# The first load of wq as 16 whole rows, the other 112 rows by columns

## The chip, the cores and the metric

The kernel runs on one core of a Trainium2 chip. Time is device microseconds (us) of that core, from the program's start to its end; the figure for a kernel is the median of several runs. Beside it stands a profile, one execution recorded by the hardware profiler, whose span runs from the first instruction to the last.

## The reference

One decoding step of an attention block and a small MLP in parallel, on one token x of 512 numbers, all in float32:

```
xn = layernorm(x)
q  = xn @ wq                                  # 512 x 4096, 32 heads of 128
scores = q . k_cache * 128 ** -0.5            # 8 kv heads, 65536 positions, 4 q heads share a kv head
o  = softmax(scores) . v_cache
y  = x + o @ wo + relu(xn @ w1) @ w2          # wo 4096 x 512, w1 512 x 1792, w2 1792 x 512
```

k_cache and v_cache hold 268 MB each; wq and wo hold 8.4 MB each, w1 and w2 3.7 MB each. Nearly all of the work is to bring them into the core once.

## The kernel before

The caches are cut into 32 chunks of 16384 positions, four to a kv head. A chunk of k is a tile `kt` of 128 partitions with rows of 64 KB, a chunk of v the like tile `vt`. TensorE multiplies a chunk of k by the four q heads (L313), VectorE transposes the scores out of the accumulator (L366) and finds their maximum, ScalarE takes exponentials (L256), and TensorE multiplies by v (L292). There is one `kt` and one `vt`, so that k comes in while v is used and the other way round.

All large loads are issued by SyncE in one order, written out by hand: wq, w1, the first k, then v and k in turn, then wo, w2 and the store. Before each k and v SyncE takes a count from a semaphore (`kfree`, `vfree`) that says that the tile is free. The rows of a load are shared out over 16 DMA engines, and each engine takes what is queued for it in order.

The projection q = xn @ wq uses the path of the scores: wq is laid out as a tile of 128 partitions with rows of 16384 numbers (64 KB) and is loaded into `kt`; the normalized x, laid out over 128 partitions, stands in `qpad` as the weights. wq comes in three loads by columns, of 4096, 4096 and 8192 columns (`WQ_CUTS`), each over all 128 partitions. Each adds 16 to a semaphore of its own when all of it has landed (`WQ_SEMS`):

- the first adds to `ends`. GpSimd computes the end of the layernorm (L208 to L212), takes 16 from `ends` (L213), then copies xn to `qpad` and releases TensorE through `q` (L214);
- the second adds to `k`, for which TensorE waits (L308) before the eight rounds of matmuls of the loop at L309. A round is 2048 columns, so rounds 0 and 1 use the first load, 2 and 3 the second, 4 to 7 the third;
- the third adds to `wq2`. VectorE waits for it after its first transpose (L367 to L368) and only then lets TensorE go on to rounds 4 to 7. With the last transposes it also adds to `kfree` (L365), so that SyncE can issue the first k into the same tile (L161, L162).

The first load (L151) is issued ahead of the section in which the engines run by their own semaphores; the others (L157 to L159) follow inside it, after a meeting of the engines. w1 (L160) stands behind them; GpSimd multiplies and adds it up (L217 to L224), for TensorE's sums at L281. The vector x itself comes in by ScalarE's own queue (L234, L235), in 128 rows of 16 bytes and one row of 2 KB, through the same DMA engines.

Of the kernel before, what the change touches and what calls it, by code (L numbers as in the profile page):

```python
# [40 lines left out]
WQ_CUTS = [4096, 4096, 8192]  # L41
WQ_SEMS = ["ends", "k", "wq2"]
# [2 lines left out]
W2_SUM = 12  # L45
W2_ROWS = 10
PASSES = 3


def take(e, sem, n=1):  # L50

    return e.sem_inc(sem, -n).wait_op(sem, n, "sem-ge")  # L52
# [7 lines left out]
def attention_and_mlp_kernel(  # L60
# [12 lines left out]
    sp, pe, dve, act, pool = nc.sync, nc.tensor, nc.vector, nc.scalar, nc.gpsimd  # L73
    scale = float(DH) ** -0.5

    def sbuf(name, *shape):
        return nc.alloc_sbuf_tensor(name, list(shape), F32).ap()
# [3 lines left out]
    def sem(name):  # L81
        if name not in sems:
            sems[name] = nc.alloc_semaphore(name)
        return sems[name]

    def after(ins, name, n=1):

        return ins.wait_op(sem(name), n, "sem-ge")

    kt = sbuf("kt", P, CHUNK)  # L90
# [47 lines left out]
    wq_row = wq[0].rearrange("p a n -> p (a n)")  # L138
# [9 lines left out]

    load = sp.dma_start(kt[:, : WQ_CUTS[0]], wq_row[:, : WQ_CUTS[0]]).then_inc(sem(WQ_SEMS[0]), 16)  # L151
    tc.no_tile_sem_insts.add(load.ins.name)
    tc.add_to_no_dep_group("first", load.ins)
    tc.declare_fence(pool.nop().ins, group="first")
    section = ctx.enter_context(ExitStack())
    inside = section.enter_context(tc.tile_critical(sync_engine=mybir.EngineType.Pool, no_gpsimd_drain=True))  # L156
    for i in range(1, len(WQ_CUTS)):  # L157
        cut = slice(wq_at[i], wq_at[i + 1])
        sp.dma_start(kt[:, cut], wq_row[:, cut]).then_inc(sem(WQ_SEMS[i]), 16)  # L159
    sp.dma_start(wt, w1_row).then_inc(sem("w1"), 16)  # L160
    take(sp, sem("kfree"))  # L161
    sp.dma_start(kt, k[0, 0]).then_inc(sem("k"), 16)  # L162
# [8 lines left out]
    for i in range(len(WO_CUTS)):  # L171
        cut = slice(wo_at[i] * D, wo_at[i + 1] * D)
        sp.dma_start(kt[:, cut], wo_row[:, cut]).then_inc(sem(f"wo{i}" if i else "k"), 16)
    sp.wait_ge(sem("hT"), 1)
    for i in range(len(W2_CUTS)):
        cut = slice(w2_at[i] * D, w2_at[i + 1] * D)
# [7 lines left out]
    def link(ins):  # L184

        if chain[0]:
            after(ins, "pool", chain[0])
        chain[0] += 1
        return ins.then_inc(sem("pool"), 1)
# [20 lines left out]
    link(pool.tensor_scalar(st[:, 6:7], st[:, 6:7], -0.5, 1.5, op0=ALU.mult, op1=ALU.add))  # L210
    link(pool.tensor_mul(st[:, 7:8], st[:, 5:6], st[:, 6:7]))
    link(pool.tensor_scalar_mul(xn, xc, st[:, 7:8]))  # L212
    take(pool, sem("ends"), 16)  # L213
    after(pool.tensor_copy(qpad[:, :XA], xn), "pool", chain[0]).then_inc(sem("q"), 1)  # L214
    f = DFF_ALL
    w1_of = [wt[:, a * f : (a + 1) * f] for a in range(XA)]
# [54 lines left out]
    with nc.body("turns", valid_engines=[pe.engine]):  # L271
# [3 lines left out]
        with pe.If(t > 1):  # L275
            after(pe.transpose(pma[:GROUP, :P], m, ident), "d2p").then_inc(sem("p2d"), 1)  # L276
            after(pe.matmul(pmb[:, :GROUP], ones[:GROUP, :], dg, start=True, stop=True), "d2p", 2).then_inc(sem("p2d"), 1)  # L277

            with pe.Fori(0, PASSES):
                for c in range(CT):  # L280
# [175 lines left out]
```

## Time and profile before

| | |
|---|---|
| median of 3 runs | 1303.14 us (1303.03 to 1303.14) |
| span of the profiled execution | 1301.3 us, 1.8 below the median; the profile gives no other time of this execution |
| moved by DMA | 561.02 MB, mean 431 GB/s |
| DMA engines' share of the span | 99.7% |
| PE, PEld, DVE, ACT, POOL busy | 60%, 18%, 21%, 6%, 3% of the span |
| first, second and third load of wq, issued to landed | 7.2, 11.5 and 20.8 us |
| w1, issued to landed | 28.9 us |
| k and v chunks, issued to landed (median) | 24.1 and 29.3 us |

PE is TensorE's matmuls, PEld its weight loads, DVE VectorE, ACT ScalarE, POOL GpSimd, SP SyncE; SPq and ACTq are the instructions by which SyncE and ScalarE issue DMAs. A line such as `L313 PE MATMUL banks<-kt,qpad ... x32 [3.03 <-PEq L52]` gives the line of the kernel, the engine, the operation, output and inputs, how many are merged, and in brackets how long the engine had been idle and what ended that. The DMA share and the GB/s of a window count a row by the time at which it starts.

### The profile page before, as it was taken

The numbers are of one execution on the slowest core, as the hardware profiler recorded it, in microseconds if no ns is written. First come the engines' busy times: TensorE is split into PE (matmuls) and PEld (weight loads), VectorE is DVE, ScalarE is ACT, GpSimd is POOL, SyncE is SP. The second block draws the span as 40 slices with busy tenths as digits, with TensorE's granted clock in tenths as the row PEclk, the third lists the DMA queues.
The fourth block names the chain that finished last, engine by engine and source line by source line (L and its number), as shares of the span: only waits on it lengthen the run. The fifth ranks groups of instructions, "written<-read, shape, count | busy, mean of one in ns | idle before, by whom it ended". The sixth has DMA issues, their size and how long they took to land.

```text
span 1301.3 us, 13055 instructions
## 1 busy us (share of the span) xinstructions
PE 774.9 (60%) x5474; PEld 231.1 (18%) x5474; DVE 274.8 (21%) x466; ACT 76.2 (6%) x299; POOL 34.8 (3%) x30
## 2 busy tenths in 40 slices
PE   3365674665576456566555566666567466557557
PEld 1111121111121111121111121111112111112112
DVE  2211222211222220222220122221122221122222
ACT  1000000000000000000000000000000000000000
POOL 1900000000000000000000000000000000000000
PEclk9677877776887777786776777677777777777779
DMA  9999999999999999999999999999999999999998
GB/s 403 451 419 451 419 451 419 435 435 419 451 419 451 419 451 419 449 421 423 447 419 451 419 451 419 451 419 435 435 419 451 419 451 419 451 419 443 427 420 370
DMA packets 11236, 561.02 MB, mean 431 GB/s; under 512 B 1505, under 2 KB 1505, under 8 KB 1890
## 3 DMA queue, kind: packets, MB, share of 16 engines
q1 hardware_dynamic: 11088, 561.00, 99.7%
q10 hardware_dynamic: 146, 0.00, 0.0%
q8 instruction: 1, 0.02, 0.0%
q14 instruction: 1, 0.01, 0.0%
HBM read 560.99 MB, written 0.00 MB: 431 GB/s over the span
## 4 chain that ended last, share of the span: by engine, by line
issue 94%; DMA 3%; POOL 2%; SPq 0%; PE 0%; DVE 0%; POOLq 0%
DMA wt<-w 3%; POOL wt L219 1%; POOL wt L224 0%; POOL wt L222 0%; POOL wt L223 0%; SPq L177 0%; SPq L159 0%; PE banks L339 0%; DVE ysb L417 0%; SPq L151 0%; POOL hT L226 0%; SPq L452 0%; POOLq L156 0%
## 5 line engine op out<-in xcount | busy, mean ns | idle before, releaser
L313 PE MATMUL banks<-kt,qpad 128*32 128x512 f32 x2176 | 310.0, 733 | 311.1 <-PEq L52 308.7
L292 PE MATMUL banks<-vt,probs 128*16 128x512 f32 x2048 | 271.3, 690 | 82.1 <-PEq L52 82.1
L366 DVE STREAM_TRANSPOSE tr<-banks 128x1024 f32<-128x1024 f32 x136 | 170.0, 1250 | 471.4 <-PE banks L313 466.8
L313 PEld LDWEIGHTS banks<-kt,qpad 128*32 128x32 f32 x2176 | 84.5, 131 | 509.6 <-issue 496.3
L281 PE MATMUL banks<-wt,ones 128*1 128x448 f32 x768 | 121.3, 786 | 0.0
L292 PEld LDWEIGHTS banks<-vt,probs 128*16 128x16 f32 x2048 | 68.4, 108 | 298.4 <-issue 298.4
L392 DVE COPY o_sb<-banks 128x512 f32<-128x512 f32 x32 | 22.1, 692 | 455.3 <-PE banks L292 455.3
L254 ACT ACTIVATE corr<-diff 128x8 f32<-128x8 f32 x32 | 6.7, 208 | 1179.8 <-ACTq L52 1179.8
L256 ACT ACTIVATE probs<-tr,nb_new 128x128 f32<-128x128 f32 x128 | 65.3, 521 | 0.0
L276 PE MATMUL banks<-ident,m 128*4 128x128 f32 x32 | 9.7, 303 | 78.9 <-DVE m L384 78.9
L302 PE MATMUL banks<-sel,o_sb 128*128 128x4 f32 x256 | 32.8, 252 | 18.7 <-PEq L52 18.7
L302 PEld LDWEIGHTS banks<-sel,o_sb 128*128 128x128 f32 x256 | 31.0, 191 | 20.6 <-issue 20.6
L226 POOL TENSOR_SCALAR hT<-ysum 128x14 f32<-128x14 f32 x1 | 0.3, 257 | 1220.7 <-DVE ysum L404 1220.7
L384 DVE TENSOR_REDUCE m<-tr 128x4 f32<-128x512 f32 x32 | 32.2, 1006 | 2.9
L281 PEld LDWEIGHTS banks<-wt,ones 128*1 128x1 f32 x768 | 20.2, 100 | 58.9 <-issue 58.4
L277 PE MATMUL banks<-dg,ones 4*128 4x4 f32 x64 | 15.4, 309 | 20.0 <-DVE dg L387 20.0
L256 ACT ACTIVATION_READ_ACCUMULATOR probs<-tr,nb_new 128x1 f32 x128 | 24.0, 187 | 0.0
L276 PEld LDWEIGHTS banks<-ident,m 128*4 128x4 f32 x32 | 2.6, 81 | 108.0 <-DVE m L384 108.0
L219 POOL TENSOR_SCALAR wt<-wt,xn 128x1792 f32<-128x1792 f32 x4 | 19.1, 4797 | 16.5 <-DMA wt<-w 16.5
L277 PEld LDWEIGHTS banks<-dg,ones 4*128 4x128 f32 x64 | 12.6, 245 | 27.1 <-DVE dg L387 27.1
L299 PEld LDWEIGHTS banks<-part_sum,ones 128*128 128x128 f32 x64 | 9.5, 188 | 27.2 <-issue 27.2
L395 DVE TENSOR_TENSOR lo_run<-lo_run,banks 128x8 f32<-128x8 f32 x32 | 5.2, 163 | 40.0 <-DVEq L52 40.0
(69 smaller groups left out, 91.1 us busy)
## 6 DMA issues: line engine op xcount, KB each, us to landing
kt<-wq SPq DMA_DIRECT2D x2, 2048.0 KB, 9.3
kt<-wq SPq DMA_DIRECT2D x1, 4096.0 KB, 20.8
kt<-wo SPq DMA_DIRECT2D x1, 4096.0 KB, 15.5
kt<-wo SPq DMA_DIRECT2D x2, 2048.0 KB, 22.2
wt<-w SPq DMA_DIRECT2D x1, 3584.0 KB, 28.9
wt<-w SPq DMA_DIRECT2D x1, 1536.0 KB, 9.5
wt<-w SPq DMA_DIRECT2D x1, 1024.0 KB, 11.7
kt<-k SPq DMA_DIRECT2D x32, 24.1
```

What stands on the lines that cost most here:

```text
L219: last = pool.tensor_scalar_mul(w1_of[a], w1_of[a], xn[:, a : a + 1])
L256: last = act.activation(probs[:, :, g], tr[:, :, g], AF.Exp, bias=nb_new[:, g : g + 1], scale=scale, accum_out=part_sum[:, g : g + 1],)
L276: after(pe.transpose(pma[:GROUP, :P], m, ident), "d2p").then_inc(sem("p2d"), 1)
L277: after(pe.matmul(pmb[:, :GROUP], ones[:GROUP, :], dg, start=True, stop=True), "d2p", 2).then_inc(sem("p2d"), 1)
L281: ins = pe.matmul(hrow[32 * c : 32 * c + 1, :], ones[:, :1], hb[:, :, 32 * c : 32 * c + 32], start=True, stop=True,)
L292: last = pe.matmul(acc[c : c + WIDE * GROUP, :], probs[:, b : b + WIDE, :].rearrange("p b g -> p (b g)"), vt[:, b * DH : (b + WIDE) * DH], ...
L299: pe.matmul(lo_new[:, 0, :], ones, part_sum, start=True, stop=True).then_inc(sem("vfree"), 1)
L302: last = pe.matmul(lo_new[:, 1, :], o_sb[:, b, :], sel[:, b, :], start=(b == 0), stop=(b == WIDE - 1),)
L313: last = pe.matmul(pair[s // 2 % 2][32 * c : 32 * c + 32, s % 2 * 512 : s % 2 * 512 + 512], qpad, kb[:, s * 16 : s * 16 + 16, c, :], start ...
L366: ins = after(dve.transpose(tr2[:, s * 1024 : (s + 1) * 1024], pair[s % 2]), "p2d", s + 1)
L384: dve.reduce_max(m, tr.rearrange("p b i -> p i b")[:, :GROUP, :], axis=AX.X).then_inc(sem("d2p"), 1)
L392: after(dve.tensor_copy(o_sb.rearrange("p b d -> p (b d)"), acc), "p2d", 7).then_inc(sem("d2p"), 1)
```

## The change

The first load takes 16 whole rows: partitions 0 to 15 of `kt` with all 16384 columns, 64 KB each, 1 MB in all. The three loads by columns remain, with the same cuts, but bring only partitions 16 to 127. The first of them is issued inside the section, in front of the two others, and adds to `ends` as well, from which GpSimd now takes 32. All of wq still comes in once, into the same places.

```diff
+FIRST = 16
...
-    load = sp.dma_start(kt[:, : WQ_CUTS[0]], wq_row[:, : WQ_CUTS[0]]).then_inc(sem(WQ_SEMS[0]), 16)
+    load = sp.dma_start(kt[:FIRST, :], wq_row[:FIRST, :]).then_inc(sem(WQ_SEMS[0]), 16)
     tc.no_tile_sem_insts.add(load.ins.name)
...
+    sp.dma_start(kt[FIRST:, : WQ_CUTS[0]], wq_row[FIRST:, : WQ_CUTS[0]]).then_inc(sem(WQ_SEMS[0]), 16)
     for i in range(1, len(WQ_CUTS)):
         cut = slice(wq_at[i], wq_at[i + 1])
-        sp.dma_start(kt[:, cut], wq_row[:, cut]).then_inc(sem(WQ_SEMS[i]), 16)
+        sp.dma_start(kt[FIRST:, cut], wq_row[FIRST:, cut]).then_inc(sem(WQ_SEMS[i]), 16)
...
-    take(pool, sem("ends"), 16)
+    take(pool, sem("ends"), 32)
```

On SyncE, at the start of the program, these are the loads before, with the partitions and columns of each and the semaphore that it waits for:

```order
L151 DMA kt<-wq 128x4096
L452 UNCONDITIONAL_BRANCH [waits Pool_sequencer_49]
L159 DMA kt<-wq 128x4096
L159 DMA kt<-wq 128x8192
L160 DMA wt<-w 128x7168
L162 DMA kt<-k 128x16384 [waits kfree]
```

And these are the loads after (the lines of the changed kernel, one or two further down):

```order
L152 DMA kt<-wq 16x16384
L454 UNCONDITIONAL_BRANCH [waits Pool_sequencer_49]
L158 DMA kt<-wq 112x4096
L161 DMA kt<-wq 112x4096
L161 DMA kt<-wq 112x8192
L162 DMA wt<-w 128x7168
L164 DMA kt<-k 128x16384 [waits kfree]
```

One load stands more between the meeting and w1, and four loads of wq are ahead of w1 in place of three. No other engine has an instruction more, fewer or elsewhere.

## The prediction

> **What bounds the kernel now.** I read the page's DMA part first, then the stream between the first and the last chunk, then the first 60 us by engine queue. The second column of the queue line is MB moved, the third the share of the time of sixteen DMA engines:
>
> ```profile
> DMA packets 11236, 561.02 MB, mean 431 GB/s; under 512 B 1505, under 2 KB 1505, under 8 KB 1890
> q1 hardware_dynamic: 11088, 561.00, 99.7%
> ```
>
> SyncE's queue q1 moves all of the 561 MB and keeps the sixteen engines busy for 99.7% of the span. The same view for the stretch from 60 to 1260 us, where only k and v move, has one rate from slice to slice:
>
> ```profile
> GB/s 419 443 430 419 454 419 446 428 419 454 419 450 424 419 454 419 450 424 419 454 419 452 422 419 454 419 452 422 419 454 419 452 422 419 454 419 452 422 419 454
> DMA packets 8928, 520.10 MB, mean 433 GB/s; under 512 B 992, under 2 KB 992, under 8 KB 992
> q1 hardware_dynamic: 8928, 520.10, 100.1%
> ```
>
> There is no idle time in the middle that could absorb a delay from the start. What the stream loses in its first microseconds arrives at the end whole; what it wins there as well. So the question is how long the first 12 MB (wq, then w1) take. The timeline of SyncE's queue (start, duration, instruction) and the wait chain's w1 piece (start, duration):
>
> ```profile
> 0.73 0.39 SPq L151 DMA_DIRECT2D kt<-wq  x1
> 1.34 0.83 SPq L159 DMA_DIRECT2D kt<-wq  x2
> 2.22 0.69 SPq L160 DMA_DIRECT2D wt<-w  x1
> 26.46 0.33 SPq L162 DMA_DIRECT2D kt<-k  x1
> 27.18 0.34 SPq L165 DMA_DIRECT2D vt<-v  x1
> 2.22 28.86 DMA wt<-w
> ```
>
> w1 lands at 2.22 + 28.86 = 31.08 us. The first k chunk is issued at 26.46, 4.6 us before that, so the stream does not stop between them. The first line below is the landing time of that k issue (last three figures), the second TensorE's first weight load on it:
>
> ```profile
> DMA to landing us min/median/max: 24.0/24.0/24.0
> 50.53 0.44 PEld L313 LDWEIGHTS banks<-kt,qpad 128*32 128x32 f32 x8 [25.17 <-issue]
> ```
>
> k lands at 50.46, 19.4 us after w1. A chunk is 128 rows of 64 KB, eight to an engine, so **one engine takes 19.4 / 8 = 2.42 us for a row of 64 KB** and 0.61 for one of 16 KB. The stream's start, in windows (length, then the busy times of PE, PEld, DVE, ACT and POOL, clock, DMA share, GB/s):
>
> ```profile
> 0.00:1.70 1.70, 0.00 (x0) 0.00 (x0) 0.17 (x1) 0.00 (x0) 0.76 (x9) 1.00 0.00 0
> 1.70:6.70 5.00, 0.00 (x0) 0.00 (x0) 3.47 (x1) 1.28 (x1) 1.50 (x8) 1.00 0.98 370
> ```
>
> No data row starts before 1.70 us, 1.0 after the first issue; the next 5 us run at 370 GB/s, 5 x (1 - 370/433) = 0.7 us behind the later pace. These 1.7 us are all that a better start could win.
>
> **The change part by part.** *The first load* was 128 rows of 16 KB (2 MB) and becomes 16 rows of 64 KB (1 MB), partitions 0 to 15 of `kt`, one per engine. Floor: each engine writes its row at its own pace, 2.42 us, and nothing is lost. But no row of this trace shows a large load to fewer than 128 partitions. The even rate of about 433 GB/s, whatever is loaded, says that something fixed and evenly divided holds the stream, and the receiving side may be that as well as the engines: sixteen paths into the memory with eight partitions each fit the rows just as well. Then sixteen neighbours lie on fewer paths than sixteen engines. Ceiling: eight neighbours to a path, two paths, 8 x 2.42 = 19.4 us, the time of a whole chunk. The steps between are two to a path (4.8 us) and four (9.7 us). The trace cannot choose. I take four: it is one step from the ceiling, whose row is the only one here in which 64 KB rows fill a set of partitions, and two from the floor, for which there is only the rate of an engine that has a path to itself. Cost 9.7 - 2.42 = **7.3 us**; ends 0 and 17.0. If four rows share a path evenly, all sixteen engines are held, and nothing behind them on the queue starts earlier, since an engine takes its rows in order.
>
> The Trainium skill, SBUF — State Buffer, section on the DMA port swizzle, says that 16 ports receive DMA writes, that partitions 0 to 15 reach 4 of them, and gives 104 GB/s measured for 1 MiB to these partitions. By it the 1 MiB would take 10.1 us, and the term be 7.7 us. No row of before shows such a load.
>
> *The other 112 rows* come in three loads by columns: 7 rows to each engine instead of 8, 7 x 2.42 = 16.9 us at full pace. Floor: 16.9, so that the whole of wq takes 2.42 + 16.9 = 19.4 as before. With paths, a share of seven consecutive rows no longer coincides with one path: shares start at 16, 23, 30 and so on, straddle two sets of four or more, and at any moment some engines meet on a path and others have one alone. A row met by one other engine takes twice as long. Ceiling: the slowest engine meets another on all seven rows, +16.9; floor 0. A middle can be counted: the partitions 16, 23, 30, ... 121 that sixteen engines write first fall into sets of four that are mostly different, yet those engines that meet stay together for some rows, since both move on by one partition at a time, and an engine that falls behind then meets the w1 rows of those ahead. The load counts only when its slowest engine is done. I take half of the slowest engine's rows as met: 16.9 x 1.5 - 16.9 = **8.5 us**, nearest to neither end.
>
> *The queue.* One issue more on SyncE, 0.33 to 0.44 us by the rows of L159 to L162; w1 is then issued at about 2.6. That is covered: the 16-row load, from 1.7 us on, keeps each engine busy until 4.1 at the earliest, and the 112-row load is issued at 1.34 as L159 was, so its rows are there at 2.4. If the cover were gone, 0.4 us. The next issue, k at 26.46, waits for `kfree` in any case. GpSimd's wait for the first load now wants 32 in place of 16, no instruction more; behind it stand its copy of xn to `qpad` and TensorE's first matmuls, so their cover is to be looked at. First the load of x among the DMA issues (KB, us to landing), then the timeline:
>
> ```profile
> xT<-x ACTq DMA_DIRECT2D x1, 2.0 KB, 8.2
> ```
>
> ```profile
> 9.27 0.21 ACT L240 ACTIVATE xc<-xT 128x4 f32<-128x4 f32 x1 [6.03 <-DMA xT<-x]
> 14.52 0.19 POOL L214 COPY qpad<-xn 128x4 f32<-128x4 f32 x1
> 15.00 5.17 PE L313 MATMUL banks<-kt,qpad 128*32 128x512 f32 x32 [3.03 <-PEq L52]
> 22.66 1.25 DVE L366 STREAM_TRANSPOSE tr<-banks 128x1024 f32<-128x1024 f32 x1 [2.90 <-DMA kt<-wq]
> 26.45 1.25 DVE L366 STREAM_TRANSPOSE tr<-banks 128x1024 f32<-128x1024 f32 x1 [0.58 <-PE banks L313]
> ```
>
> x lands at 9.2 us, and TensorE has the first half of wq done at 20.2; then VectorE waits for the third load, until 22.66, and 3.8 us later SyncE issues k. Its 2 KB take 8.2 us, so I take it that its eight short rows per engine take turns with wq's rows. With a 64 KB row of 9.7 us ahead they begin at 1.7 + 9.7 = 11.4 and need eight turns of 0.61 to 1.22 us: x lands at 16.3 to 21.2, TensorE is done 20.2 - 9.2 = 11.0 later, at 27.3 to 32.2. The third load lands at 11.4 + 16.9 = 28.3 with no meetings and 36.8 with my half. So x's chain stays hidden behind the third load, by a microsecond or more. k follows 3.8 us after that load, and w1 still streams for 31.08 - 22.6 = 8.5 us behind it: the slowest engine does not run dry (8.5 against 3.8 + 1.0), and engines ahead of it only idle.
>
> *Sum*: 7.3 + 8.5 = 15.8 us. The profiled span of 1301.3 becomes 1317.1; the median of the runs, 1303.14, lies 1.8 above the span and becomes **1318.9**. The likeliest case's own range follows from the second term's ends: 1303.1 + 7.3 = 1310.4 to 1303.1 + 7.3 + 16.9 = 1327.3.
>
> **The rivals.** *No sharing (not slower).* The engines are the bound, and each writes its row at 2.42 us wherever it goes. For it: 433 GB/s is equally well sixteen engines at 27 GB/s. Against it: nothing in the trace, only that it needs the receiving side to have room to spare. It decides from the point where the 16-row load's last row ends by 4.2 us. Time: 1303.1, or down to 1301.4 if all 1.7 us of the start were won; that is 0.13%, below the 0.2% (2.6 us) that a measurement of this kernel can tell from no change. So faster is nearly excluded.
>
> *Eight rows to an engine.* 112 = 14 x 8: if the loads keep eight rows to an engine, two engines idle and fourteen have nine rows of 64 KB: +2.42 us, 1305.6. For it: eight is what every load has now. The Trainium skill, DMA: Bandwidth & Descriptors, section on why a DMA increments its semaphore by 16, says that the largest count up to 16 that divides the rows is used, which gives 16 engines with seven rows; no row of before shows it.
>
> *Rows dealt one by one.* If row i goes to engine i mod 16, all engines write to sixteen neighbours at each moment, and all of wq comes at the pace of four paths: 4 x 19.4 = 77.6, +58.2, 1361.3. The trace gives no partition of a single row, so nothing speaks for it or against it but that contiguous shares are simpler.
>
> *Two to a path.* The first load takes 4.8 (+2.4), the meetings a quarter of the rows (+4.2): 1309.7.
>
> **How the numbers follow.** Sharing by four with contiguous shares 0.73, two to a path 0.07, one by one 0.07, no sharing 0.10, eight to an engine 0.03. The last two count as within 0.2%, but for 0.01 of a won start and a tail of the 1305.6 above the bound: slower 0.87, same 0.12, faster 0.01. The range 1306 to 1328 holds the first two cases and leaves out no sharing, eight to an engine and one by one, 0.2 in all.
>
> **What would show it.** The window of the first 10 us: about 110 GB/s after 1.7 us if four share, still about 370 if none do. The landing of the first load: 9.7 us or more after its first row, against 2.4. x's landing near 16 to 21 us instead of 9.2. The third load's landing, VectorE's wait for it and the issue of k all later by the same 14 to 16 us, and w1's landing near 47; from there on every row as before, only shifted, with the stream at 433 GB/s. If x's chain and not the third load ends VectorE's wait, my cover was wrong; if w1's and k's landings are more than 20 us apart, the slowest engine ran dry. The prediction is wrong if partitions 0 to 15 take rows as fast as any, or if seven-row shares never meet, or meet nearly always.

## The result and the profile after

The changed kernel takes 1323.06 us, median of 5 runs (1322.65 to 1325.13), against 1303.14 (1303.03 to 1303.83) before: 1.0153 times as long, 95% interval 1.0141 to 1.0166, or 19.9 us more. The profiled execution's span went from 1301.3 to 1320.9 us, 19.6 more.

The page of the changed kernel, its DMA part:

```profile
DMA packets 11220, 561.02 MB, mean 425 GB/s; under 512 B 1521, under 2 KB 1521, under 8 KB 1906
q1 hardware_dynamic: 11072, 561.00, 99.6%
```

The bytes are the same and the engines are still reckoned busy for 99.6% of the span, but at 425 GB/s. An engine that is held up on the way into the memory counts as busy: over the first ten microseconds of data below, from 1.7 to 11.7 us, the share comes to 1.08 (the mean of 1.72 and 0.45) and the rate to 131 GB/s. The stretch from 80 to 1280 us shows where the loss is not:

```profile
GB/s 448 424 424 448 424 441 433 424 443 426 441 433 428 439 426 439 435 424 443 426 439 435 424 443 426 439 435 426 441 426 439 435 424 443 426 439 435 424 446 424
DMA packets 8928, 520.10 MB, mean 433 GB/s; under 512 B 992, under 2 KB 992, under 8 KB 992
```

433 GB/s, as before. So all of it is in the start, which the windows show (the last figure is GB/s by the rows that start in a window):

```profile
1.70:6.70 5.00, 0.00 (x0) 0.00 (x0) 3.47 (x1) 1.28 (x1) 1.51 (x8) 1.00 1.72 210
6.70:11.70 5.00, 0.00 (x0) 0.00 (x0) 0.00 (x0) 0.00 (x0) 0.00 (x0) 1.00 0.45 53
11.70:16.70 5.00, 1.17 (x4) 1.00 (x4) 0.00 (x0) 1.44 (x9) 0.00 (x0) 1.00 0.88 246
16.70:21.70 5.00, 0.00 (x0) 0.00 (x0) 0.16 (x1) 1.89 (x3) 1.26 (x6) 1.00 1.02 282
21.70:26.70 5.00, 0.11 (x4) 0.14 (x8) 0.00 (x0) 0.00 (x0) 0.00 (x0) 1.00 1.08 279
26.70:31.70 5.00, 4.80 (x32) 1.14 (x31) 1.25 (x1) 0.00 (x0) 0.00 (x0) 1.00 1.04 295
31.70:36.70 5.00, 0.00 (x0) 0.00 (x0) 0.00 (x0) 0.00 (x0) 0.00 (x0) 0.93 1.00 256
```

The sixteen rows of the first load all start in the first window (210 GB/s over 5 us is 1.05 MB) and then nothing starts until 9.8 us. In the trace's records of single rows these sixteen took 8.0 to 9.3 us each, and the last ended 9.6 us after the first had begun; an engine with a free way takes 2.42. Then come 25 us of the 112-row loads at 246 to 295 GB/s in place of 433. None of their rows runs at full pace: those of 16 KB take 0.75 to 2.50 us, half of them over 0.95, in place of 0.61, and those of 32 KB take 2.0 us in the median, in place of 1.21. The timeline, with the answers to the rows quoted of before:

```profile
0.73 0.40 SPq L152 DMA_DIRECT2D kt<-wq  x1
1.35 0.32 SPq L158 DMA_DIRECT2D kt<-wq  x1
1.73 1.11 SPq L161 DMA_DIRECT2D kt<-wq  x2
2.88 0.44 SPq L162 DMA_DIRECT2D wt<-w  x1
13.38 0.20 ACT L242 ACTIVATE xc<-xT 128x4 f32<-128x4 f32 x1 [10.14 <-DMA xT<-x]
19.82 0.19 POOL L216 COPY qpad<-xn 128x4 f32<-128x4 f32 x1 [1.26 <-POOLq L53]
26.59 4.91 PE L315 MATMUL banks<-kt,qpad 128*32 128x512 f32 x32 [10.51 <-PEq L53]
40.97 6.25 PE L315 MATMUL banks<-kt,qpad 128*32 128x512 f32 x32 [9.46 <-DVEq L370]
41.01 1.25 DVE L368 STREAM_TRANSPOSE tr<-banks 128x1024 f32<-128x1024 f32 x1 [9.90 <-DMA kt<-wq]
47.42 0.35 SPq L164 DMA_DIRECT2D kt<-k  x1
49.35 19.12 POOL L221 TENSOR_SCALAR wt<-wt,xn 128x1792 f32<-128x1792 f32 x4 [29.34 <-DMA wt<-w]
70.13 0.46 PEld L315 LDWEIGHTS banks<-kt,qpad 128*32 128x32 f32 x8 [23.84 <-issue]
```

VectorE's wait for the third load ends at 41.0 in place of 22.7 (+18.3). w1 has landed at 49.3 (2.88 and 46.4 to landing) in place of 31.1 (+18.2). The first k is there at 70.0 in place of 50.5 (+19.5), and from there nothing is lost or won to the end. So the 19.6 us divide into 7.1 for the first load (9.56 - 2.42), about 11.1 for the 112-row loads (18.2 - 7.1), and a third part of 1.3 that opens between w1 and k: they land 20.7 us apart, where 19.4 is the time of a chunk.

### The profile page after: what moved, and what is told of

The parts are those of the page before. It is cut to its first block, busy times and chain, and to the rows that moved or that the text cites. A ratio compares the mean times of both kernels' runs of the same rounds, so it can differ in the third digit from the quotient of the medians.

```text
span 1320.9 us, 13056 instructions
## 1 busy us (share of the span) xinstructions
PE 772.9 (59%) x5474; PEld 231.0 (17%) x5474; DVE 279.1 (21%) x466; ACT 76.1 (6%) x299; POOL 34.9 (3%) x30
## 3 DMA queue, kind: packets, MB, share of 16 engines
q1 hardware_dynamic: 11072, 561.00, 99.6%
## 4 chain that ended last, share of the span: by engine, by line
issue 92%; DMA 5%; POOL 2%; SPq 0%; PE 0%; DVE 0%; POOLq 0%
DMA wt<-w 5%; POOL wt L221 1%; POOL wt L226 0%; POOL wt L225 0%; POOL wt L224 0%; PE banks L341 0%; SPq L161 0%; SPq L179 0%; DVE ysb L419 0%; SPq L152 0%; PE banks L354 0%; SPq L158 0%; POOL hT L228 0%; SPq L454 0%; POOLq L157 0%
## 5 line engine op out<-in xcount | busy, mean ns | idle before, releaser
L283 PE MATMUL banks<-wt,ones 128*1 128x448 f32 x768 | 116.5, 759 | 0.0
L304 PE MATMUL banks<-sel,o_sb 128*128 128x4 f32 x256 | 32.8, 251 | 18.7 <-PEq L53 18.7
L304 PEld LDWEIGHTS banks<-sel,o_sb 128*128 128x128 f32 x256 | 31.0, 191 | 20.5 <-issue 20.5
L386 DVE TENSOR_REDUCE m<-tr 128x4 f32<-128x512 f32 x32 | 32.2, 1005 | 2.9
L283 PEld LDWEIGHTS banks<-wt,ones 128*1 128x1 f32 x768 | 20.0, 98 | 54.3 <-issue 53.7
L279 PE MATMUL banks<-dg,ones 4*128 4x4 f32 x64 | 14.4, 293 | 19.9 <-DVE dg L389 19.9
## 6 DMA issues: line engine op xcount, KB each, us to landing
wt<-w SPq DMA_DIRECT2D x1, 3584.0 KB, 46.4
wt<-w SPq DMA_DIRECT2D x1, 1536.0 KB, 11.7
```

Of the source, the lines that this page charges most:

```text
L283: ins = pe.matmul(hrow[32 * c : 32 * c + 1, :], ones[:, :1], hb[:, :, 32 * c : 32 * c + 32], start=True, stop=True,)
L304: last = pe.matmul(lo_new[:, 1, :], o_sb[:, b, :], sel[:, b, :], start=(b == 0), stop=(b == WIDE - 1),)
L386: dve.reduce_max(m, tr.rearrange("p b i -> p i b")[:, :GROUP, :], axis=AX.X).then_inc(sem("d2p"), 1)
```

## The experiments

### Is it the partitions that make the 16-row load slow?

Each of these kernels is the one before with one load more (one of the three lines marked c16, s4 and s8), behind w1, into the idle tile `vt`, where it is never used; SyncE waits for it ahead of the first v. Source and size of the three are the same, and only the sixteen partitions written differ. This kernel and the others with a load added to the kernel before were executed once each; the kernel before, executed beside them, took 1302.9 to 1303.8 us, so that differences of several microseconds are clear.

```diff
     sp.dma_start(wt, w1_row).then_inc(sem("w1"), 16)
+    sp.dma_start(vt[0:16, :], wq_row[0:16, :]).then_inc(sem("extra"), 16)       # c16
+    sp.dma_start(vt[0:64:4, :], wq_row[0:16, :]).then_inc(sem("extra"), 16)     # s4
+    sp.dma_start(vt[0:128:8, :], wq_row[0:16, :]).then_inc(sem("extra"), 16)    # s8
     take(sp, sem("kfree"))
     sp.dma_start(kt, k[0, 0]).then_inc(sem("k"), 16)
+    sp.wait_ge(sem("extra"), 16)
```

> The kernel before with one load more, issued behind w1 and ahead of the first k: 16 rows of 64 KB of wq into partitions 0 to 15 of vt, whose content is never used. By the sharing theory (four neighbouring partitions to one receiving path) the load takes 4 x 2.42 = 9.7 us of the stream: it lands 9.7 us after w1, k 29 us after w1 in place of 19.4, and the span is 1301.3 + 9.7 = 1311.0. By the rival that the slow first load was an effect of the program's start, and not of the partitions, it takes 2.4 us and the span is 1303.7.

> As c16, the same 16 rows of wq, but into partitions 0, 4, 8 ... 60. If sets of four neighbours have a path each and no two sets share one, every row has a path to itself: 2.4 us, span 1303.7. If a partition and the one 32 further on share a path, two rows meet: 4.8 us, 1306.1. If eight neighbours share a path, two rows meet as well: 4.8 us. If the source, one block of 1 MB in memory, was what was slow, it takes 9.7 us as c16, 1311.0.

> As c16, the same 16 rows of wq, but into partitions 0, 8, 16 ... 120. If eight neighbours share a path, or four do and no two sets share, each row has a path to itself: 2.4 us, span 1303.7. If sets of four 32 apart share a path (but not those 64 apart), two rows meet: 4.8 us, 1306.1. If all sets 32, 64 and 96 apart share one, four rows meet: 9.7 us. If the source was what was slow, 9.7 us, 1311.0.

The landing of the added load after its issue at 2.9 us, in c16, s4 and s8:

```profile
DMA to landing us min/median/max: 38.0/38.0/38.0
```

```profile
DMA to landing us min/median/max: 33.5/33.5/33.5
```

```profile
DMA to landing us min/median/max: 33.8/33.8/33.8
```

w1 landed at 31.1 us before, so the added load took 9.8 us in c16 (2.9 + 38.0 - 31.1), 5.3 in s4 and 5.6 in s8. The records of the sixteen rows, from the first start to the last end, give 9.5, 5.3 and 5.6. The spans are 1311.3, 1307.1 and 1306.9 us, 10.0, 5.8 and 5.6 more than before. The start of the program has no part in it, since this load comes 30 us into the run; nor has the source, which is the same. What counts is where the rows go: neighbours in sets of four share a path, and sixteen rows spread over the partitions still meet in pairs. In s4 no two rows are in one set of four, so either eight neighbours share a path or sets do. s8 excludes eight neighbours, which would have taken 2.4 us; it allows pairs of sets 32 apart, but not all sets 32, 64 and 96 apart.

### Which sets share a path

The same added load with 64 rows, four to an engine, at three starts:

```diff
+    sp.dma_start(vt[0:64, :], wq_row[0:64, :]).then_inc(sem("extra"), 16)       # r64_0
+    sp.dma_start(vt[32:96, :], wq_row[0:64, :]).then_inc(sem("extra"), 16)      # r64_32
+    sp.dma_start(vt[36:100, :], wq_row[0:64, :]).then_inc(sem("extra"), 16)     # r64_36
```

> As r112, but 64 rows into partitions 0 to 63, four whole rows to an engine, so that each engine's share is one set of four neighbours. Without sharing, or if no two sets share a path: 4 x 2.42 = 9.7 us. If a set and the one 32 further on share a path, two engines meet on each path all the time: 19.4 us, lands 19.4 after w1, span 1320.7. If rows were dealt one by one: 38.7 or more.

> As r64_0, the same 64 rows of wq, but into partitions 32 to 95. If a set of four shares a path with the set 32 further on (0 to 31 with 32 to 63, 64 to 95 with 96 to 127), these sixteen sets have sixteen paths: 9.7 us, lands 9.7 after w1, span 1311.0, half of r64_0. If it's sets 64 apart that share, this one and r64_0 both take 9.7; if a load of 64 rows is slow for its count of rows, both take 19.4.

> As r64_32, the same 64 rows of wq, four to an engine, but one set of four further on, into partitions 36 to 99. If all that counts is that two rows in flight are on one path, fourteen engines write at 2.42 us a row, and only the two whose sets are 64 to 67 and 96 to 99 meet, at 4.8 to 5.1: the stream runs near 400 GB/s for the first 9.7 us of the load, and the slowest engine ends 19.4 to 20.5 us after w1, span about 1321.5. If each engine has a path of its own, and every row to another path than the engine's own is slow, all engines are slow, and the stream runs at 210 to 230 GB/s for all of the load, about 20 us, span about 1322 as well: the rate in the windows tells them apart.

Windows of r64_0, then r64_32, then r64_36:

```profile
35.00:40.00 5.00, 0.00 (x0) 0.00 (x0) 0.00 (x0) 0.00 (x0) 5.00 (x2) 0.50 1.02 210
40.00:45.00 5.00, 0.00 (x0) 0.00 (x0) 0.00 (x0) 0.00 (x0) 5.00 (x2) 0.50 1.02 210
```

```profile
35.00:40.00 5.00, 0.00 (x0) 0.00 (x0) 0.00 (x0) 0.00 (x0) 5.00 (x2) 0.50 1.12 485
40.00:45.00 5.00, 0.00 (x0) 0.00 (x0) 0.00 (x0) 0.00 (x0) 5.00 (x2) 0.50 1.15 498
```

```profile
35.00:40.00 5.00, 0.00 (x0) 0.00 (x0) 0.00 (x0) 0.00 (x0) 5.00 (x2) 0.50 1.01 393
40.00:45.00 5.00, 0.00 (x0) 0.00 (x0) 0.00 (x0) 0.00 (x0) 5.00 (x2) 0.50 1.20 367
45.00:50.00 5.00, 0.00 (x0) 0.00 (x0) 0.00 (x0) 0.00 (x0) 5.00 (x2) 0.50 1.24 367
50.00:55.00 5.00, 0.00 (x0) 0.00 (x0) 0.00 (x0) 0.00 (x0) 4.92 (x3) 0.50 0.53 184
```

The same 4 MB run at half the pace into partitions 0 to 63 and at full pace into 32 to 95 (a window counts whole rows at their start, hence figures above 433). The landings, 48.8 and 38.0 us after the issue at 2.9, are 20.6 and 9.8 us behind w1's 31.1; spans 1322.2 and 1311.5. So a set of four shares its path with the set 32 further on, and 32 to 95 is a stretch in which no two do: sixteen paths in all, eight partitions to each. The Trainium skill, SBUF — State Buffer, section on the DMA port swizzle, has this map, with 0 to 63 on eight ports. It agrees with these six runs, r64_36 included; for its 196 GB/s, measured with 1 MiB into 64 partitions, 204 stand here (4.19 MB in 20.6 us).

r64_36 was to tell whether a path belongs to an engine, and it does not. The trace names no engine for a row; I follow an engine from the end of one row to the start of the next. Fourteen of the engines write their rows at 2.4 to 2.8 us, though with four rows to each in order none of them is on the set that it had in r64_32. Only two engines, by the map those with sets 64 to 67 and 96 to 99, take 4.5 to 5.1. That part came as expected, with 393 GB/s in the first full window. The end did not: the load lands 26.0 us behind w1 (2.9 + 54.2 - 31.1), not 19.4 to 20.5, and the span is 1328.5. In the records of rows the two late engines go on into a time in which others already load k, a third engine comes onto their path, and three rows at once take 7.1 to 8.1 us each. So the two that were late were made later by one that was ahead.

### Why the 112-row loads are slow

```diff
+    sp.dma_start(vt[16:128, :], wq_row[0:112, :]).then_inc(sem("extra"), 16)    # r112
+    sp.dma_start(vt[0:112, :], wq_row[0:112, :]).then_inc(sem("extra"), 16)     # r112_0
+    sp.dma_start(vt[32:128, :], wq_row[0:96, :]).then_inc(sem("extra"), 16)     # r96_32
```

> The kernel before with one load more behind w1: 112 rows of 64 KB of wq into partitions 16 to 127 of vt, whose content is never used. At full pace it takes 7 x 2.42 = 16.9 us and lands 16.9 us after w1. By the theory that shares of seven rows meet on the paths, whatever was ahead of them, it lands 25 to 29 us after w1 (the changed kernel took 28.5), and the span is 1301.3 + 25 to 29. By the rival that the meetings in the changed kernel came from the engines being staggered by its first load, it lands 17 to 20 us after w1, span 1318 to 1321. Rows dealt one by one would take 68 us.

> As r112, the same 112 rows of wq, but into partitions 0 to 111. If it is the start at 16 that makes all shares meet, this takes less than r112's 34.8 us; if a share of seven rows is what does it, since it fits no set of four wherever it starts, it takes 30 to 36 us again, span 1331 to 1337. Full pace would be 16.9 us, 1318.2.

> As r112 and r64_32, but 96 rows into partitions 32 to 127, six to an engine. Full pace is 6 x 2.42 = 14.5 us behind w1, span 1315.8. If any share that is not one whole set of four is slow as the shares of seven were (34.8 us, 2.06 times full pace), it takes 25 to 30 us, span 1326 to 1331. If only an odd share is slow, it takes 14.5 to 17 us.

The windows of r112, and then the landing in r96_32:

```profile
35.00:40.00 5.00, 0.00 (x0) 0.00 (x0) 0.00 (x0) 0.00 (x0) 5.00 (x2) 0.50 1.05 288
40.00:45.00 5.00, 0.00 (x0) 0.00 (x0) 0.00 (x0) 0.00 (x0) 5.00 (x2) 0.50 0.79 236
45.00:50.00 5.00, 0.00 (x0) 0.00 (x0) 0.00 (x0) 0.00 (x0) 5.00 (x2) 0.50 0.93 223
50.00:55.00 5.00, 0.00 (x0) 0.00 (x0) 0.00 (x0) 0.00 (x0) 4.92 (x2) 0.50 1.12 249
```

```profile
DMA to landing us min/median/max: 58.6/58.6/58.6
```

r112's load lands 32.8 us behind w1's 31.1 (2.9 + 61.0 - 31.1), r112_0's 32.2 (3.0 + 60.3), r96_32's 30.4 (2.9 + 58.6), against 16.9, 16.9 and 14.5 at the full pace of the engines. The spans are 1335.6, 1334.5 and 1332.3. The rival falls: without any late load ahead, with all engines in step, 112 rows run at half that pace, and worse than in the changed kernel. Neither the start at 16 nor the odd share matters, since six rows to an engine from partition 32 are as slow. r112 comes out above what was expected, r112_0 within it and r96_32 a little above. (The 34.8 us that the last two expectations give for r112 is not its landing, which is 32.8.)

Part of this follows from the map. The sixteen partitions left out in r112 or r112_0 lie on four paths and halve those; the other twelve paths still get eight rows each. In r96_32 eight paths still get eight. At 2.42 us a row, none of the three loads can take less than 8 x 2.42 = 19.4 us, the time of a whole chunk, however its rows are dealt. That is an estimate from the map, and 11 to 13 us of the three times stay above it.

What was not expected is how even it is. In r96_32 every row of every engine takes 4.3 to 5.1 us, from the first to the last; in r112 all sixteen first rows take 4.3 to 4.8. If engine e had rows 6e to 6e + 5 or 7e to 7e + 6 of the load, as in the forecast, only two pairs in each would have met at the start by the map that the loads of 64 rows show, and the others would have had 2.42. So either the rows of these loads are not dealt in such consecutive shares, or something slows them that the map does not have; the place of the rows in the source, for one, was not varied here. Dealing one by one, with four rows to a path, is excluded by its 9.7 us a row. If two engines took neighbouring rows side by side, every row would meet one other: 6 x 4.84 = 29.0 us for r96_32, which fits its rows, and 7 x 4.84 = 33.9 for r112, which fits in total, but not its third and fourth rows, 2.7 to 3.5 us on fourteen of the engines. The trace does not give a row's partition, and no run tells how they are dealt. It stays open.

### The first load alone

```diff
-    load = sp.dma_start(kt[:, : WQ_CUTS[0]], wq_row[:, : WQ_CUTS[0]]).then_inc(sem(WQ_SEMS[0]), 16)
+    load = sp.dma_start(vt[:16, :], wq_row[:16, :]).then_inc(sem(WQ_SEMS[0]), 16)
...
+    sp.dma_start(kt[:, : WQ_CUTS[0]], wq_row[:, : WQ_CUTS[0]]).then_inc(sem(WQ_SEMS[0]), 16)
     for i in range(1, len(WQ_CUTS)):
...
-    take(pool, sem("ends"), 16)
+    take(pool, sem("ends"), 32)
```

> The changed kernel's first part alone: the first load is 16 rows of 64 KB of wq into partitions 0 to 15 (of vt, where they are not used), and behind it wq comes in by three loads over all 128 partitions as before, so that 1 MB is loaded twice. By the theory that the change's cost is 7.1 us of sharing in the first load and some 11 us of the 112-row loads, this one costs the first load alone, 9.6 us: w1 lands at 40.7 in place of 31.1, the span is 1310.9, the time 1312.7, and 1.3 us more if k comes late behind w1 as in the changed kernel. By the rival that the late first load unsettles the engines, whatever follows it, so that the loads behind it slow down as they did in the changed kernel, w1 lands near 50 and the time is near 1322.

1313.16 us (1312.60 to 1314.17), 1.0076 times before (1.0059 to 1.0093); span 1312.4. w1 lands at 40.8 (issued at 3.0, 37.8 to landing), k 20.7 us later, at 61.5. The rival falls: behind the slow first load, loads of 128 rows run as they always did. Of the 11.1 us in the span, 9.7 are there when w1 lands, and 1.3 come up between w1 and k, as in the changed kernel. The profiled execution is the longest of the four; two others have spans of 1310.8 and 1310.9 us, what the first load costs alone. They have no trace, so whether k was on time in them is not known.

### The late k

In the changed kernel SyncE issues k 6.4 us after the third load's wait ends (47.42 against 41.01), before 3.8 (26.46 against 22.66). In between are TensorE's rounds 4 to 7, which take 6.25 us in place of 3.64, and TensorE's granted clock is the reason that the windows offer (changed kernel; the clock is the third figure from the end):

```profile
31.00:36.00 5.00, 0.50 (x8) 0.00 (x0) 0.10 (x1) 0.00 (x0) 0.00 (x0) 1.00 1.03 269
36.00:41.00 5.00, 0.03 (x4) 0.03 (x5) 0.00 (x0) 0.00 (x0) 0.00 (x0) 0.50 0.91 275
41.00:46.00 5.00, 5.00 (x24) 1.15 (x28) 2.50 (x2) 0.00 (x0) 0.00 (x0) 0.50 1.01 436
46.00:48.00 2.00, 1.22 (x12) 0.20 (x4) 0.59 (x1) 0.00 (x0) 0.00 (x0) 0.93 0.67 287
```

TensorE ends the first half at 31.5, and from 36 on the clock is 0.50, while it waits; the second half begins at that clock. Before, the wait was from 20.2 to 22.6, and the clock stayed at 1.00:

```profile
19.00:22.00 3.00, 1.17 (x12) 0.14 (x4) 0.76 (x1) 0.00 (x0) 0.00 (x0) 1.00 1.01 436
22.00:27.00 5.00, 3.64 (x32) 0.96 (x32) 3.05 (x3) 0.00 (x0) 0.00 (x0) 1.00 0.95 407
```

The Trainium skill, TensorE: Matmul & The Clock Gate, section on the HAM clock gate, says that half the clock is the state after an idle window of about 3.4 us, and full clock comes after a busy one. The 4.5 us until the fall agree with that, but the fall does not always take 3.4 us of idling: in the kernel before, TensorE ends its second half at 26.3, and the clock falls at 28.4.

That the late issue costs time shows in the records of rows. w1's last rows end on the sixteen engines between 47.4 and 48.7 us; k's first rows start only at 48.4 to 49.7, so most engines stood idle, and these rows then took 2.9 to 3.5 us in place of 2.42. In first16 k was late in the same way: issued 6.5 us after the third load's wait ended (38.97 against 32.43), with the clock at 0.61 in the window from 30 to 35 us. Two runs bear on it:

```diff
+    sp.dma_start(vt[:, :4096], wq_row[:, :4096]).then_inc(sem("extra"), 16)     # cover, behind w1
...
+            if s == ROUNDS // 2:                                                # busy, TensorE's loop of rounds
+                with pe.If(t < 1):
+                    for _ in range(36):
+                        pe.matmul(acc[:16, :P], ident[:, :16], ident, start=True, stop=True)
```

In cover SyncE also waits for the added load ahead of the first v, as in the runs above.

> The changed kernel with a load of 128 rows of 16 KB (2 MB, 4.84 us of the stream) into vt more, behind w1 and ahead of the first k, never used. If k came late in the changed kernel, since TensorE's half clock put off its issue until w1's cover was used up, the longer cover takes that back: k lands 19.4 us after the added load, which lands 4.8 after w1, so the span is 1320.9 + 4.8 - 1.3 = 1324.4. If k was not late but slow for another reason (its first rows took 2.9 to 3.5 us in place of 2.42), it is late again: k lands 20.7 us after the added load, and the span is 1325.7.

> The changed kernel, with 36 matmuls of 128 columns more on TensorE (into rows of acc that the next chunk writes anew) in the first turn, between rounds 3 and 4, while it waits for the third load of wq. If TensorE's half clock is why SyncE issued k 6.4 us after that load had landed, in place of 3.8, then a busy TensorE keeps the clock at 1.00, k is issued 3.8 to 4.2 us after the landing, lands 19.4 us after w1 in place of 20.7, and the time falls by about 1.3 us from the changed kernel's 1323.1. If the late k has another cause, it lands 20.7 us after w1 as before and the time stays.

In busy the same windows read as the first fence shows, and the timeline around the issue of k as the second:

```profile
31.00:36.00 5.00, 5.00 (x52) 3.65 (x43) 0.86 (x1) 0.00 (x0) 0.00 (x0) 1.00 0.99 252
36.00:41.00 5.00, 4.18 (x39) 3.47 (x36) 0.00 (x0) 0.00 (x0) 0.00 (x0) 1.00 0.90 227
41.00:46.00 5.00, 3.50 (x32) 0.96 (x32) 2.50 (x2) 0.00 (x0) 0.00 (x0) 1.00 1.00 424
```

```profile
42.54 1.25 DVE L372 STREAM_TRANSPOSE tr<-banks 128x1024 f32<-128x1024 f32 x1 [10.68 <-DMA kt<-wq]
46.34 0.35 SPq L164 DMA_DIRECT2D kt<-k  x1
```

The clock stays at 1.00, k is issued 3.8 us after the wait's end, and lands 19.4 us after w1 (46.34 + 23.7 = 70.0 against 3.0 + 47.6 = 50.6); its first rows take 2.42 us. So it was the clock that made k late in the profiled execution. The median, 1321.18 us, is 1.9 below the changed kernel's 1323.06, but the ratios to before, 1.0136 (1.0119 to 1.0153) and 1.0153 (1.0141 to 1.0166), overlap: the time alone would not show it. Busy's profiled execution is the longest of its four (span 1323.7, the others 1319.1 to 1319.4); its third load landed 1.5 us later than the changed kernel's, so the 112-row loads do not take the same time in every execution.

In cover k lands at 73.1 us, 19.4 after the added load's 53.7 (3.4 + 50.3), so with a longer cover the late issue costs nothing there either. But the span is 1326.0, not 1324.4: from k's landing to the end it takes 2.0 us longer than the changed kernel, 1.2 of them for the final store, which took 2.6 us to land in place of 1.4; the rest is not accounted for. The time, 1327.71 us (1326.87 to 1333.06), tells nothing apart.

## Why the prediction was right

Slower was forecast, at 1318.9 us in a range of 1306 to 1328, and 1323.06 was measured. Its steps:

- *The first load, +7.3 us by four rows to a path*: right. It measured 7.1, and c16, s4 and s8 show that it is the set of four partitions that does it. The choice of four among one, two, four and eight was not backed by a row of before: as an argument from the trace, its being right was luck. The rows of after and the added loads now stand for it. No sharing (2.4 us) and two to a path (4.8) fall with c16.
- *The 112-row loads, +8.5*: the right sign and within its ends, too small: about 11.1. The step that failed is the count of meetings. Consecutive shares of seven with half of the slowest engine's rows met was the forecast, and that they meet nearly always was named as a sign that the prediction is wrong. They do: in the changed kernel all 16 KB rows of these loads take over 0.7 us in place of 0.61, and alone, from engines in step, the loads run at half pace on every engine (r112), which consecutive shares do not explain by the map. So the forecast came near for the size of this term, not for its reason. Its floor of 0 was wrong too, by the prediction's own picture of sixteen paths with eight partitions each: sixteen neighbours on four paths leave eight rows on each of the others, 19.4 us in place of 16.9, so at least 2.5 of the 11.1 were certain once four share. In the changed kernel, where the first load leaves the engines out of step, they took 28.0 us (16.9 + 11.1), less than r112's 32.8. That the engines' being out of step is what helps there is an argument, not shown.
- *The queue's cover, +0*: wrong by 1.3 us. I set w1's 8.5 us, counted to its landing, against 3.8 from the third load to k and 1.0 to its first row. With the longer wait TensorE fell to half clock, 3.8 became 6.4, and 6.4 + 1.0 = 7.4 were needed. w1's rows lasted only 6.4 to 7.7 us past the end of the wait (47.4 to 48.7 against 41.0), for they end 0.6 to 1.9 us ahead of the landing at 49.3. The sign that I had named for this, w1 and k more than 20 us apart, is what the profile shows. That a wait also lowers TensorE's clock was the missing link.
- *x's chain hidden behind the third load*: right in the result. x landed at 13.3 us, earlier than my 16.3 to 21.2; its short rows did not take turns with rows of 16 KB one by one, but ran together between 9.8 and 11.5 us, behind the first load's. GpSimd's copy then waited for wq and not for x, and TensorE for the second load of wq (26.4).
- *Nothing given back or lost later*: right; 433 GB/s from 80 to 1280 us, and the 19.5 us at k's landing are the 19.6 at the end.
- *The rivals*: eight rows to an engine would have cost 2.4 us, and one by one 58; neither is in the measured 18.2 at w1. The 1.7 us of the start that a better first load could win were not won: the first row of data still starts 1.0 us after the issue.

The sum was 15.8 against 19.6: 0.2 too much in the first term, 2.6 and 1.3 too little in the others.

No version here beats the kernel before. Of the loads tried, only those to all 128 partitions and to the 64 from 32 on ran at full pace.

## What to carry to other kernels

For a kernel bound by its loads, count what a load writes to: 128 partitions at once, or 64 from 32 to 95, use all the paths into the memory here; 16 neighbours use a quarter of them, 0 to 63 half. Count the rows on the fullest path: a load to 96 or 112 partitions has eight there, as many as one to 128, and took 30 to 33 us where the 128 take 19.4. Sixteen large rows, one per DMA engine, look like full use of the engines, and the busy share says so too; look at GB/s and at the time of a single row. And when a stage waits longer than before, look up whether the work behind the wait still runs at the same clock.

## What was not expected of the hardware

- Loads of 96 and 112 rows run at half pace on all sixteen engines, row after row (4.3 to 5.1 us for 64 KB in r96_32), where consecutive shares would have met in two pairs only.
- While a path has three rows in flight, others are slower as well: in r64_36, while three engines were at 7.1 to 8.1 us a row, the rows of k of the other thirteen took 3.0 us in place of 2.42, and from 40 to 55 us the windows average 306 GB/s in place of 433.
- Single slow rows come up long after the start: in the changed kernel twelve rows of k and v after the first 60 us take 2.6 to 3.7 us, the last at 1055 us, where before not one of 8192 rows took over 2.6. That the engines are still out of step would explain it, but is not shown.
